# Two maxima over partitions taken by a diagonal, a product with ones and a row maximum; weight splits of small experts moved between three engines

## The chip, the cores and the metric

The kernel runs on one core of a Trainium2 chip. The metric is device time in microseconds of one execution. Engines are named as the profile names them: PE (matrix products; PEld is its weight load), DVE (vector), ACT (scalar), POOL (GpSimd) and SP, whose queue issues most transfers. An engine with a q behind it is its sequencer.

## The reference, cut to what matters

Three stages follow each other: attention with a learned position bias, a mixture of eight experts of which each token takes one, and a dense pair of products.

```python
# attention: B, H, S, D = 2, 8, 576, 64; hidden of the bias = 32
scores = scale * q @ k.T
x = log1p(|i - j|) / log1p(max(i, 1))
scores += (relu(x * w1 + b1) @ w2)            # one bias per head, same for both batches
attn = softmax(scores) @ v
# experts: 1152 tokens of 512, 8 experts, hidden 1024, capacity 288 tokens
e = argmax(x @ w_gate); gate = softmax(x @ w_gate)[e]
y = relu(x_e @ w1[e]) @ w2[e]                 # each expert on its own tokens
out = gate * y
# dense pair, hidden 2048
h = out @ w_in
g = where(h >= 1, h, where(h <= -1, 0, (h + 1)**2 / 4))
return g @ w_out
```

## The kernel before

**The bias, first row block.** A hidden unit of the bias is a kink in x. The kernel turns each kink into a threshold, compares distances with thresholds (`mask_step`, line 244, DVE), and multiplies the masks with two small fp16 tables on PE (`ab_mm`, lines 262 and 263). Of a chunk, DVE scales one half by the table of x (`ab_x`, line 268); ACT copies the other half out (`ab_bs`, line 276, four buffers) and POOL adds it (`ab_add`, line 281), or DVE does both (`ab_stt`, line 286). Each block of 128 rows has 18 chunks. The first block stands alone ahead of the attention, in a loop over `c`; the later blocks are mixed into the attention.

**Two power-of-two scales.** `pow2_scale` takes a maximum over all 128 partitions and turns it into a power of two and its inverse in six small DVE steps. It is called twice. The first call (`sab`) scales the fp16 tables: nothing of the bias can begin before it. Its input `am` is a row maximum of a 128x16 tile (line 619). The second (`sv`) scales v into fp16. Its input `vsum` is made in round 8 of the chunk loop, from three row maxima that ACT takes of v (`v_abs`, line 179); its steps are dealt out over the next rounds. In both, `partition_all_reduce` on POOL (line 117) takes the maximum.

**Around it.** The order on each engine is that of the program text. The constants `cst` (with the unit matrix `ident`), the thresholds' row `lrow`, the distances `sD`, the table `xtab`, and q, k and v are loaded at the start by queues of SP and ACT. After the first scale, DVE scales `lrow` (line 630), ACT takes its exponential and scales `sD` (lines 631 and 632), ACT rounds part of k (`k_hi`, line 153) and POOL takes the rest (`k_lo`, line 159); then come the first mask and the first product.

**The experts.** A weight chunk is 128x1024 values; an expert has eight, four of w1 and four of w2, counted through as `n`. Every chunk is split into a rounded part (`w_hi`) and the rest (`w_lo`, line 888), each in a ring of six. The rounding is a copy on ACT (line 883), for chunks 1 and 3 of each eight on DVE (line 881). The rest is on DVE for even chunks and on POOL for odd ones. `w_lo` also issues the load of chunk `n + 6` on SP's queue. Products take three terms of the two parts.

Each expert has two arms, and the number of its tokens chooses. `small_arm` (at most 128 tokens; lines 1129 and 1140) computes with the tokens stationary, transposes h and y (lines 1116 and 1157), and calls `hook(s)` eight times: `hook(s)` splits chunk 8e + 4 + s, so s = 0 to 3 are this expert's w2 (chunks 4 to 7 of the eight) and s = 4 to 7 the next expert's w1 (chunks 0 to 3). Between hooks 6 and 7 stands `mid()`, where `x_pick` (lines 1179 and 1180, DVE) copies the next expert's tokens to `xsh` and `xsl`; the next small expert's first product waits for these. `wide_arm` (lines 1089 and 1103) takes all 288 columns. In this trace experts 0, 1 and 4 take the wide arm, 2, 3, 5, 6 and 7 the small one.

Of the kernel before, what the change touches and what calls it, by code (L numbers as in the profile page):

```python
# [9 lines left out]
F32 = mybir.dt.float32  # L10
# [6 lines left out]
ALU = mybir.AluOpType  # L17
AX = mybir.AxisListType.X
# [21 lines left out]
    "pp": [12, 10],  # L40
    "HV": (1, 3),
}

P = 128
# [6 lines left out]
def tile_attn_moe_moe2(  # L51
# [6 lines left out]
    nc = tc.nc  # L58
# [14 lines left out]
    const = ctx.enter_context(tc.tile_pool(name="const", bufs=1))  # L73
# [9 lines left out]
    ap1 = attn.enter_context(tc.tile_pool(name="ap1", bufs=1, reuse_waits="tile"))  # L83
# [5 lines left out]
    psM = attn.enter_context(tc.tile_pool(name="psM", bufs=2, space=PSUM, reuse_waits="tile"))  # L89
# [8 lines left out]
    ident = cst[:, 24:24 + P]  # L98
# [8 lines left out]
    def late_consts():  # L107
# [4 lines left out]
        nc.sync.dma_start(out=wg, in_=a["moe_w_gate"].rearrange("(k p) e -> p k e", p=P))  # L112
        nc.sync.dma_start(out=iota, in_=a["c_iota"])

    def pow2_scale(m1, name, pool):
        amax = ap1.tile([P, 1], F32, name=name + "_m")
        nc.gpsimd.partition_all_reduce(amax, m1, P, bass_isa.ReduceOp.max)
        ei = ap1.tile([P, 4], I32, name=name + "_e")
        ef = ap1.tile([P, 4], F32, name=name + "_f")
        sc = const.tile([P, 2], I32, name=name + "_s")  # L120
        s = sc.bitcast(F32)
        steps = [
            lambda: nc.vector.tensor_single_scalar(out=ei[:, 0:1], in_=amax.bitcast(I32), scalar=23, op=ALU.logical_shift_right),
            lambda: nc.vector.tensor_copy(ef[:, 0:1], ei[:, 0:1]),
            lambda: nc.vector.tensor_scalar(out=ef[:, 1:2], in0=ef[:, 0:1], scalar1=64.0, scalar2=-14.0, op0=ALU.max, op1=ALU.add),
            lambda: nc.vector.tensor_scalar(out=ef[:, 2:3], in0=ef[:, 1:2], scalar1=-1.0, scalar2=254.0, op0=ALU.mult, op1=ALU.add),
            lambda: nc.vector.tensor_copy(ei[:, 1:3], ef[:, 1:3]),
            lambda: nc.vector.tensor_single_scalar(out=sc, in_=ei[:, 1:3], scalar=23, op=ALU.logical_shift_left),
        ]
        return s[:, 1:2], s[:, 0:1], steps  # L130

    FH = G["fh"]
    kst = {h: ap1.tile([P, B, S], F32R, name=f"kst{h}") for h in range(H) if h // 2 not in FH}
# [61 lines left out]
    def q_load(it, hp):  # L195
        if hp in FH:
            qraw[it, hp] = ap3.tile([P, 2, P], F32, tag="qf", name="qf")
            nc.sync.dma_start(out=qraw[it, hp], in_=a["qf"][it, hp])
            return
        qraw[it, hp] = ap3.tile([P, 2, B, P], F32, tag="qraw", name="qraw")  # L200
        nc.sync.dma_start(out=qraw[it, hp], in_=a["q"][it, :, 2 * hp:2 * hp + 2])
# [92 lines left out]
    def ab_ev(it, c, dve=False):  # L294
        if dve:
            ab_stt(it, c)
        else:
            ab_bs(it, c)
            ab_add(it, c)
# [292 lines left out]
    with tc.manual_schedule():  # L592
# [9 lines left out]
            nc.sync.dma_start(out=vraw[:, 3 * c:3 * c + 3, :], in_=a["v"][:, 3 * c:3 * c + 3, :])  # L602
        k_load(2)
        q_load(0, 1)
        nc.vector.memset(run, 0.0)
        warm = ap1.tile([P, 1], F32, name="warm")
        nc.vector.memset(warm, 0.0)
# [4 lines left out]
        am = ap1.tile([P, 1], F32, name="am")  # L612
# [4 lines left out]
        V.tensor_scalar(out=ab[:, 1, :], in0=w2r, scalar1=wcol[:, 1:2], scalar2=None, op0=ALU.mult)  # L617
        V.tensor_scalar(out=sg[:, 0:1], in0=sg[:, 0:1], scalar1=-1.0, scalar2=None, op0=ALU.add)
        V.tensor_reduce(out=am, in_=abf, axis=AX, op=ALU.max, apply_absolute_value=True)
        sa, isa, wsteps = pow2_scale(am, "sab", const)  # L620
        V.tensor_scalar(out=sg[:, 1:2], in0=wcol[:, 0:1], scalar1=sg[:, 0:1], scalar2=1e-30, op0=ALU.mult, op1=ALU.max)
        V.reciprocal(out=sg[:, 2:3], in_=sg[:, 1:2])
        wsteps[0]()
        V.tensor_scalar(out=sg[:, 3:4], in0=sg[:, 2:3], scalar1=sg[:, 0:1], scalar2=-1.0, op0=ALU.mult, op1=ALU.mult)
        wsteps[1]()
# [38 lines left out]
        for c in range(NCK + 1):  # L664
            if c < NCK:
                ab_mm(0, c, wide=c % 4 >= 2)
            if 1 <= c <= NCK:
                (ab_xp if G["evx"][c - 1] else ab_x)(0, c - 1)
            if c + 2 < NCK:
                mask_step(0, c + 2)  # L670
            if 1 <= c <= NCK:
                ab_ev(0, c - 1, dve=c in EVD)
            if c in G['va']:
                v_abs(G['va'].index(c))
            if c == 8:
                vsum = ap1.tile([P, 1], F32, name="vsum")
                V.tensor_reduce(out=vsum, in_=vm[:, 0:3], axis=AX, op=ALU.max)
                sv, _, vsteps = pow2_scale(vsum, "sv", const)
                vst["s"] = sv
                vsteps.append(lambda: V.tensor_copy(cvec, sv))  # L680
            if c > 8:
                for f in vsteps[2 * (c - 9):2 * (c - 9) + 2]:
                    f()
            if c == G['pp'][0]:
                v_hi(0)
            if c == G['pp'][1]:
                k_hi(2)
            if c == 1:
                q_hi(0, 0)
                q_lo(0, 0)  # L690
            if c == 8:
                q_hi(0, 1)
            if c == 12:
                late_consts()
                xtab_load(1)
# [133 lines left out]
    NR, NS = 6, 6  # L829
# [44 lines left out]
            w2_dma(n - NCH)  # L874

    HV = G.get('HV', ())

    def w_hi(n):
        if n < NCH:
            if n >= NR and n % 8 in HV:  # L880
                nc.vector.tensor_copy(ring_h[n % NR], stage[n % NS])
            else:
                nc.scalar.copy(out=ring_h[n % NR], in_=stage[n % NS])  # L883

    def w_lo(n, eng=None):
        if n < NCH:
            eng = eng or (nc.gpsimd if n % 2 else nc.vector)
            eng.tensor_tensor(out=ring_l[n % NR], in0=stage[n % NS], in1=ring_h[n % NR].bitcast(F32), op=ALU.subtract)  # L888
            if n < 4:
                pass  # L890
            elif n + NS < NCH:
                w_dma(n + NS)
            elif n % 2:
                w_dma(NCH + (n + NS - NCH) // 2)

    def w_split(n):
        w_hi(n)
        w_lo(n)

    def w1_at(e, c):  # L900
        n = 8 * e + c
# [53 lines left out]
    with tc.manual_schedule():  # L955
# [34 lines left out]
        for n in range(3):  # L990
            w_hi(n)
# [170 lines left out]

    with tc.manual_schedule():
        w_hi(3)
        w_lo(3, nc.gpsimd)
        for n in range(2, 4):
            w_dma(n + NS)
        if CAP == 0:
            zfill_y()
        zx_at = min([e for e in range(E) if e * CAP + WIN > NT], default=E) if CAP else E  # L1170
        if zx_at == 0:
            zfill_x()

        def guess(e):
            if e < E and CAP > P:
                tc.mark_branch_hint_location(f"arm{e}", hint=many[e], engines=[mybir.EngineType.PE])

        def x_pick(r):
            nc.vector.tensor_copy(xsh, xTh[:, :, ds(r["dve"], P)].bitcast(F32))  # L1179
            nc.vector.tensor_copy(xsl, xTl[:, :, ds(r["dve"], P)].bitcast(F32))  # L1180

        done = nx0
        if CAP > 0:
            x_pick(regs[0])
            guess(0)
        for e in range(E if CAP > 0 else 0):
            r = regs[e]
            need = min(NTT, -(-min(NT, (e + 1) * CAP + WIN) // P))
            pre = list(range(NA, nx0)) if e == 0 else []
            more = list(range(done, need))  # L1190
            for t in more:
                if t not in xb:
                    xb[t] = x_gather(t)
            done = max(done, need)

            def hook(s, e=e):
                n = 8 * e + 4 + s
                if n < NCH:
                    w_split(n)
                if NCH - 1 <= n < NCH + 1:  # L1200
                    for k in (0, 1) if n < NCH else (2, 3):
                        w2_decode(0, k)

            def first(pre=pre):
                for t in pre:
                    x_block(t, xb[t])

            def mid(late=True, e=e, first=first, more=more, nxt=regs[e + 1] if e + 1 < E else None):
                if late:
                    first()  # L1210
                for t in more:
                    x_block(t, xb[t])
                if e + 1 == zx_at:
                    zfill_x()
                if e == 1:
                    zfill_y()
                if nxt is not None:
                    x_pick(nxt)

            if CAP > P:  # L1220
                with tc.If(cnts[e] < P + 1, preferred_fallthrough_block=False, label=f"arm{e}") as few:
                    guess(e + 1)
                    small_arm(e, r, hook, mid)
                with few.Else():
                    guess(e + 1)
                    first()
                    wide_arm(e, r, windows, hook, lambda: mid(False))
            else:
                small_arm(e, r, hook, mid)
# [40 lines left out]
    for g in range(4):  # L1270
        lim[0] = 4 * g + 5
        assert not dec or dec[0][0] > 4 * g
        for f in range(4):
            n = (NCH + 4 * g + f // 2) % NR
# [156 lines left out]
```

## Time and profile before

| | |
|---|---|
| median of 3 runs | 683.22 us (682.27 to 684.61) |
| the profiled execution | 680.61 us |
| its span, first to last instruction | 678.8 us |
| mean granted clock of PE | 0.904 of full speed |
| busy over the span | PE 579.8, DVE 501.5, ACT 360.2, POOL 354.0 us |

The first bias block runs from the start to about 50 us, the attention to about 270, the experts from about 292 to 465, the dense pair from there to the end. The profiled execution is 1.8 us longer than its span. A busy PE is not PE at its peak, since matmuls overlap. In a line of the timeline the bracket holds the idle time ahead of the first of its instructions, and what ended it.

### The profile page before, as it was taken

How to read it: one execution, taken by the hardware profiler on the slowest of the kernel's cores; microseconds unless marked ns; L12 is line 12 of the kernel's file. 1: busy time of each engine (PE TensorE's matmuls, PEld its weight loads, DVE VectorE, ACT ScalarE, POOL GpSimd, SP SyncE). 2: the span in 40 equal slices, each digit the busy share in tenths (PEclk: the TensorE clock that was granted, in tenths of full speed). 3: DMA queues.
4: the chain of work that ended last, by engine and by line, in shares of the span. 5: the costliest groups of instructions: out<-in, count | busy, mean ns of one | idle time of the engine just before them, and what ended most of it. 6: DMA issues, size and time to landing. Idle time of an engine off the chain costs nothing.

```text
span 678.8 us, 14201 instructions
## 1 busy us (share of the span) xinstructions
PE 579.8 (85%) x5332; PEld 518.2 (76%) x5332; DVE 501.5 (74%) x948; ACT 360.2 (53%) x761; POOL 354.0 (52%) x279
## 2 busy tenths in 40 slices
PE   1548887997987899499998898888989999999996
PEld 1445766876766788299998898887968988988985
DVE  3749999999989964646468854775895789787432
ACT  2446776787956854343546435543653652652720
POOL 0547998898976862455356553651330330330442
PEclk9655799899979889589999898887979999999998
DMA  9209898989976868575557754764324114200012
GB/s 334 67 3 231 162 158 141 174 153 160 171 159 129 173 109 170 185 271 176 161 190 242 244 181 150 238 207 158 125 72 176 64 63 140 106 3 0 1 47 94
DMA packets 116388, 98.26 MB, mean 145 GB/s; under 512 B 98000, under 2 KB 99024, under 8 KB 114256
## 3 DMA queue, kind: packets, MB, share of 16 engines
q1 hardware_dynamic: 114000, 89.96, 52.5%
q0 software_dynamic: 1440, 4.72, 2.0%
q10 hardware_dynamic: 864, 2.47, 1.1%
q8 instruction: 51, 0.84, 0.5%
q14 instruction: 33, 0.27, 0.1%
HBM read 65.15 MB, written 4.72 MB: 103 GB/s over the span
## 4 chain that ended last, share of the span: by engine, by line
PE 39%; DVE 6%; issue 5%; ACT 3%; POOL 2%; DMA 1%; POOLq 0%; ACTq 0%; DVEq 0%
PE psh L1287 12%; PE psy L1312 7%; PE psh L1089 6%; PE psy L1103 6%; PE psh L1312 5%; PE psh L1129 2%; POOL rl L888 2%; DMA raw<-in_moe_w_dram 1%; ACT rh L883 1%; DVE rt L923 1%; DVE rl L888 1%; DVE gl L1301 1%; DVE cl L1292 1%; POOL out_dram L1320 1%; DVE xsh L1179 1%
## 5 line engine op out<-in xcount | busy, mean ns | idle before, releaser
L888 POOL TENSOR_TENSOR rl<-raw,rh 128x1024 fp32r<-128x1024 f32 x34 | 87.9, 2587 | 94.2 <-ACT rh L883 64.8
L1297 POOL TENSOR_TENSOR rl<-rl,cl 128x384 f32<-128x384 f32 x48 | 51.4, 1071 | 137.1 <-ACT cl L1296 58.5
L262 PE MATMUL ab_ps<-Wt,mask 128*128 128x64 f16 x720 | 63.6, 208 | 53.6 <-ACT bs L276 20.6
L262 PEld LDWEIGHTS <-mask 128*128 128x128 f16 x720 | 54.5, 107 | 42.8 <-DVE mask L244 36.6
L281 POOL TENSOR_TENSOR bias<-bias,bs 128x256 f32<-128x256 f32 x78 | 71.4, 927 | 27.0 <-ACT bs L276 19.6
L392 POOL TENSOR_TENSOR hl<-s,hl 128x576 f16<-128x576 f32 x55 | 78.6, 1432 | 9.8 <-DVE hl L369 3.8
L244 DVE TENSOR_TENSOR mask<-sD,sT 128x1024 f16<-128x1024 f16 x72 | 72.9, 1026 | 0.0
L263 PEld LDWEIGHTS <-mask 128*128 128x128 f16 x720 | 55.2, 108 | 18.0 <-issue 17.9
L1287 PE MATMUL psh<-yTh,rh 128*128 128x384 f32 x192 | 66.3, 345 | 0.7 <-ACT yTh L1159 0.7
L888 DVE TENSOR_TENSOR rl<-raw,rh 128x1024 fp32r<-128x1024 f32 x30 | 47.6, 1586 | 24.5 <-ACT rh L883 16.8
L1287 PE MATMUL psh<-yTh,rl 128*128 128x384 f32 x192 | 65.7, 342 | 0.0
L1287 PE MATMUL psh<-yTl,rh 128*128 128x384 f32 x192 | 64.8, 341 | 0.0
L263 PE MATMUL ab_ps<-Wt,mask 128*128 128x64 f16 x720 | 63.3, 208 | 0.0
L883 ACT CAST rh<-raw 128x1024 fp32r<-128x1024 f32 x50 | 52.2, 1052 | 4.0 <-DMA raw<-in_moe_w_dram 2.2
L276 ACT ACTIVATE bs<-ab_ps,isa 128x256 f32<-128x256 f32 x78 | 35.3, 472 | 32.1 <-DVE bias L268 23.2
L1293 ACT ACTIVATE rl<-psh,half 128x384 f32<-128x384 f32 x48 | 28.0, 583 | 44.3 <-DVE cl L1292 44.2
L1301 DVE TENSOR_TENSOR gl<-rl,gh 128x384 fp32r<-128x384 f32 x48 | 26.8, 557 | 29.1 <-ACT gh L1300 28.6
L359 ACT ACTIVATE s<-s,mn 128x576 f32<-128x576 f32 x56 | 43.5, 776 | 1.7
L345 DVE CUSTOM_DVE_ANT_0 s<-s_ps,bias 128x576 f32<-128x576 f32 x56 | 41.8, 746 | 2.2 <-PE s_ps L317 1.4
L402 PE MATMUL mi<-V16h,pt 128*128 128x64 f16 (+1 forms) x320 | 40.3, 202 | 2.8 <-DMA pt<-hl 2.8
L268 DVE TENSOR_TENSOR bias<-ab_ps,xtab 128x256 f32<-128x256 f32 x88 | 35.6, 415 | 6.6 <-PE ab_ps L263 6.5
L402 PEld LDWEIGHTS <-pt 128*128 128x128 f16 (+1 forms) x320 | 31.4, 107 | 11.8 <-issue 4.3
(256 smaller groups left out, 1998.7 us busy)
## 6 DMA issues: line engine op xcount, KB each, us to landing
raw<-in_moe_w_dram SPq DMA_DIRECT2D x60, 512.0 KB, 4.3
raw<-in_moe_w_in_dram SPq DMA_DIRECT2D x8, 1024.0 KB, 4.8
raw<-in_moe_w_out_dram SPq DMA_DIRECT2D x8, 1024.0 KB, 4.9
qraw<-in_q_dram SPq DMA_DIRECT2D x15, 256.0 KB, 4.3
kst<-kraw SPq DMA_DIRECT2D x12, 288.0 KB, 4.0
vraw<-in_v_dram SPq DMA_DIRECT2D x3, 768.0 KB, 8.1
xd<-xt SPq DMA_DIRECT2D x8, 256.0 KB, 2.0
raw<-in_moe_w_dram ACTq DMA_DIRECT2D x4, 512.0 KB, 7.1
```

The costliest lines, as they stand in the source:

```text
L244: nc.vector.tensor_tensor(out=m, in0=win, in1=thr, op=ALU.is_gt)
L262: nc.tensor.matmul(pv[:, :, j], m[:, j, :], W["h"], start=True, stop=False)
L263: nc.tensor.matmul(pv[:, :, j], m[:, j, :], W["l"], start=False, stop=True)
L281: nc.gpsimd.tensor_tensor(out=bv, in0=bv, in1=bs_t.pop((it, c)), op=ALU.add)
L359: nc.scalar.activation(out=s, in_=s, func=AF.Exp, bias=mn[:, 1:2], scale=0.125, accum_out=st_t[it, h // 2][:, 0, h % 2, b:b + 1])
L392: eng.tensor_tensor(out=hl[:, 1, 0:S], in0=s, in1=hl[:, 0, 0:S], op=ALU.subtract)
L402: nc.tensor.matmul(o, pt[:, blk, ic], vh, start=blk == 0, stop=False)
L883: nc.scalar.copy(out=ring_h[n % NR], in_=stage[n % NS])
L888: eng.tensor_tensor(out=ring_l[n % NR], in0=stage[n % NS], in1=ring_h[n % NR].bitcast(F32), op=ALU.subtract)
L1287: nc.tensor.matmul(ps, l[:, kd, fs], mv[:, kd, cs], start=i == 0, stop=i == 11)
L1297: nc.gpsimd.tensor_tensor(out=rl, in0=rl, in1=cl, op=ALU.add)
L1312: nc.tensor.matmul(ps, l[:, tsl], mv[:, f % 2, :], start=f == 0 and i == 0, stop=f == 3 and i == 2)
```

## The change

`pow2_scale` no longer uses POOL. It multiplies the unit matrix by the column `m1` (a diagonal matrix, DVE), multiplies a matrix of ones with it on PE (every row of the product in PSUM is then the whole column), and takes the maximum of each row (DVE). These three operations are returned as a list and placed by the caller: for `sab` the first two at once and the third after two small steps; for `sv` the first in round 8, the other two in round 9, and the six steps and the copy to `cvec`, which stood in rounds 9 to 12, in rounds 10 to 12.

In the small arm the splits are dealt out anew. Rounding: only chunk 3 on DVE (before 1 and 3), the other seven on ACT. The rest: chunks 5 and 0 on POOL (before 1, 3, 5 and 7), the other six on DVE. The wide arm keeps its deal.

```diff
+    ones = ap1.tile([P, P], F32, name="ones")
+
     def pow2_scale(m1, name, pool):
         amax = ap1.tile([P, 1], F32, name=name + "_m")
-        nc.gpsimd.partition_all_reduce(amax, m1, P, bass_isa.ReduceOp.max)
+        diag = ap1.tile([P, P], F32, name=name + "_d")
+        allm = psM.tile([P, P], F32, tag="mi", name=name + "_p")
+        spread = [
+            lambda: nc.vector.tensor_scalar(out=diag, in0=ident, scalar1=m1[:, 0:1], scalar2=None, op0=ALU.mult),
+            lambda: nc.tensor.matmul(allm, ones, diag, start=True, stop=True),
+            lambda: nc.vector.tensor_reduce(out=amax, in_=allm, axis=AX, op=ALU.max),
+        ]
...
-        return s[:, 1:2], s[:, 0:1], steps
+        return s[:, 1:2], s[:, 0:1], steps, spread
...
+        nc.vector.memset(ones, 1.0)
         nc.vector.memset(run, 0.0)
...
-        sa, isa, wsteps = pow2_scale(am, "sab", const)
+        sa, isa, wsteps, wspread = pow2_scale(am, "sab", const)
+        for f in wspread[:2]:
+            f()
         V.tensor_scalar(out=sg[:, 1:2], ...)
         V.reciprocal(out=sg[:, 2:3], in_=sg[:, 1:2])
+        wspread[2]()
         wsteps[0]()
...
-                sv, _, vsteps = pow2_scale(vsum, "sv", const)
+                sv, _, vsteps, vspread = pow2_scale(vsum, "sv", const)
                 vst["s"] = sv
                 vsteps.append(lambda: V.tensor_copy(cvec, sv))
-            if c > 8:
-                for f in vsteps[2 * (c - 9):2 * (c - 9) + 2]:
+                vspread[0]()
+            if c == 9:
+                vspread[1]()
+                vspread[2]()
+            if c > 9:
+                for f in vsteps[3 * (c - 10):3 * (c - 10) + 3]:
                     f()
...
+    HVS, LPS = (3,), (5, 0)
-    def w_hi(n):
+    def w_hi(n, hv=HV):
         if n < NCH:
-            if n >= NR and n % 8 in HV:
+            if n >= NR and n % 8 in hv:
                 nc.vector.tensor_copy(ring_h[n % NR], stage[n % NS])
...
-    def w_split(n):
-        w_hi(n)
-        w_lo(n)
+    def w_split(n, few=False):
+        if few:
+            w_hi(n, HVS)
+            w_lo(n, nc.gpsimd if n % 8 in LPS else nc.vector)
+        else:
+            w_hi(n)
+            w_lo(n)
...
-            def hook(s, e=e):
+            def hook(s, e=e, few=False):
                 n = 8 * e + 4 + s
                 if n < NCH:
-                    w_split(n)
+                    w_split(n, few)
...
-                    small_arm(e, r, hook, mid)
+                    small_arm(e, r, lambda s: hook(s, few=True), mid)
```

## Rows read from the trace of the kernel before

**Rows 1.** Waits, 0 to 60 us: waiter <- releaser, us, times, longest.

```profile
ACT bs L276 <- POOL bias L281: 6.3, 3, 4.9
...
POOL bias L281 <- issue: 7.1, 1, 7.1
...
DVE sv_e L123 <- POOL sv_m L117: 6.8, 1, 6.8
...
DVE bias L268 <- PE ab_ps L263: 4.6, 2, 3.2
```

**Rows 2.** Timeline of DVE, first bias block: start, duration, line, tiles.

```profile
3.08 0.17 DVE L619 TENSOR_REDUCE am<-ab 128x1 f32<-128x16 f32 x1
...
10.84 0.15 DVE L123 TENSOR_SCALAR sab_e<-sab_m 128x1 int32<-128x1 int32 x1 [7.27 <-POOL sab_m L117]
...
11.53 0.52 DVE L630 TENSOR_SCALAR lrow<-lrow,sg 128x576 f32<-128x576 f32 x1
...
21.11 4.04 DVE L244 TENSOR_TENSOR mask<-sD,sT 128x1024 f16<-128x1024 f16 x2
...
28.88 0.15 DVE L677 TENSOR_REDUCE vsum<-vm 128x1 f32<-128x3 f32 x1 [1.06 <-ACT V16h L179]
...
49.45 0.48 DVE L286 SCALAR_TENSOR_TENSOR bias<-ab_ps,isa,bias 128x256 f32<-128x256 f32 x1
```

**Rows 3.** Instructions of lines 117 and 159, first 60 us: duration, first and last start.

```profile
L117 POOLq MODIFY_POOL_CONFIG  x4: 8/8/13, 1.5 to 30.9; - x4
...
L159 POOLq MODIFY_POOL_CONFIG  x2: 83/83/83, 11.3 to 11.4; - x2
```

**Rows 4.** Timeline of POOL, same stretch.

```profile
20.86 2.61 POOL L159 TENSOR_TENSOR kraw<-kraw 128x1152 fp32r<-128x1152 f32 x1 [9.48 <-ACT bs L276]
```

**Rows 5.** Groups of instructions by shape, whole span: count | busy us, mean ns.

```profile
L317 PE MATMUL s_ps<-kf,qf 64*128 64x288 f32 x64 | 24.3, 529 | 0.0
L473 PE MATMUL gl<-wg,extra 128*128 128x8 f32 x64 | 9.0, 267 | 0.0
...
L434 DVE TENSOR_TENSOR xt<-mi,stat 128x128 f32<-128x128 f32 x4 | 1.2, 292 | 5.7 <-PE mi L408 5.7
```

**Rows 6.** Transfers issued in the first 8 us: KB, us to landing.

```profile
xtab<-in_c_xtab_dram SPq DMA_DIRECT2D x1, 288.0 KB, 4.4
...
cst<-in_c_small_dram ACTq DMA_DIRECT2D x1, 76.0 KB, 2.0
```

**Rows 7.** Windows: length, busy PE PEld DVE ACT POOL, PE clock, DMA, GB/s.

```profile
100.00:150.00 50.00, 44.31 (x704) 36.79 (x700) 49.19 (x99) 37.42 (x98) 46.07 (x39) 0.93 0.91 163
...
429.25:446.65 17.40, 14.54 (x108) 14.09 (x108) 12.64 (x13) 9.61 (x17) 10.51 (x4) 0.90 0.73 244
...
429.10:433.00 3.90, 3.90 (x20) 3.90 (x21) 1.33 (x3) 1.20 (x2) 2.38 (x1) 0.56 0.80 268
```

**Rows 8.** Timeline of DVE, end of small expert 5.

```profile
422.23 2.44 DVE L888 TENSOR_TENSOR rl<-raw,rh 128x1024 fp32r<-128x1024 f32 x1 [0.26 <-ACT rh L883]
424.59 0.68 DVE L881 CAST rh<-raw 128x1024 fp32r<-128x1024 f32 x1
425.19 1.21 DVE L888 TENSOR_TENSOR rl<-raw,rh 128x1024 fp32r<-128x1024 f32 x1
426.33 2.56 DVE L1179 CAST xsh<-xTh 128x512 fp32r x1
```

**Rows 9.** Timeline of POOL, same stretch.

```profile
421.06 2.53 POOL L888 TENSOR_TENSOR rl<-raw,rh 128x1024 fp32r<-128x1024 f32 x1 [0.83 <-ACT rh L883]
425.41 3.20 POOL L888 TENSOR_TENSOR rl<-raw,rh 128x1024 fp32r<-128x1024 f32 x1 [1.82 <-PE psy L1140]
```

**Rows 10.** Timeline of ACT, same stretch.

```profile
421.13 2.02 ACT L883 CAST rh<-raw 128x1024 fp32r<-128x1024 f32 x2
```

**Rows 11.** Timeline of PE: first products of experts 3 and 6.

```profile
365.95 0.36 PE L1129 MATMUL psh<-rh,xsh 128*128 128x256 f32 x1 [1.70 <-DVE xsh L1179]
...
429.03 0.36 PE L1129 MATMUL psh<-rh,xsh 128*128 128x256 f32 x1 [2.58 <-DVE xsh L1179]
```

## Prediction

> **What bounds the kernel now.** I began with the waits of the first 60 us, because two of the three edits lie there. DVE waits 7.27 us for the first maximum [rows 2] and 6.8 for the second; POOL's first add behind the second waits 7.1 for nothing that the profile names, and ACT, whose four copy buffers that add should empty, waits 6.3 in all, 4.9 of it at one place; DVE then waits 4.6 for products that had no bank [rows 1]. What these waits hide shows in the instructions of lines 117 and 159: POOL's sequencer issues a MODIFY_POOL_CONFIG in front of each maximum and again when it goes back to ordinary work, and from the one at 11.3 to the first subtraction at 20.86 POOL does nothing [rows 3, 4], although ACT had rounded its input long before. So each maximum costs two loads of POOL code, one ahead of it and one behind.
>
> The reader is to see in the timeline of DVE that the whole first block hangs on that engine: `am` is there at 3.25 us, its maximum at 10.84, the block ends at 49.93 (49.45 + 0.48) [rows 2]. Then comes the attention, where DVE is busy 49.2 of 50 us and PE 44.3 [rows 7]. I see no work there tied to an absolute time: the order is that of the text, and only the first loads have a clock of their own. So I let what is won before 50 us come through to the end in full.
>
> For the third edit I read the end of small expert 5 on three engines. PE stands idle 2.58 us before expert 6, waiting for `xsh` [rows 11]. DVE makes `xsh` in 2.56 us, from 426.33 to 428.89; POOL's split ran from 425.41 to 428.61 [rows 8, 9]. The same stands at 422.23: a DVE subtraction takes 2.44 us, of which 1.36 lie before POOL's end at 423.59, and 1.08 behind it. The subtraction that met no earlier POOL split took 1.21, and POOL's split behind it 3.20 instead of about 2.4. The two engines take turns, a whole instruction at a time.
>
> **The first maximum.** Removed: a wait of 7.27 us. Added in its place, on the path: a diagonal, a product, a row maximum, and the crossings between engines. The trace of before has none of the three. The diagonal lies between 0.15 us (128x1) and 0.52 (128x576) [rows 2]; I take 0.22, nearer the small one. The fp32 product has 128 columns: 0.27 (8 columns) to 0.53 (288 columns) [rows 5], I take 0.35, which leaves room for either level of the clock. The row maximum reads 128 values from PSUM: 0.17 (16 values from SBUF) [rows 2] to 0.29 for 128x128 from PSUM [rows 5]; I take 0.27. Three crossings at 0.1 each are an estimate from the steps of the DVE chain. Sum 1.1 (0.9 to 1.7), so the six steps begin at about 4.4 instead of 10.84: 6.4 us.
>
> What would be late next are the loads. The unit matrix lands at about 2.7 (0.74 + 2.0), before `am`. `lrow` goes out on SP's queue ahead of `xtab`, which lands 4.4 us after its issue at 1.65 [rows 6], so `lrow` is there by 6.05 at the latest. Line 630, at 11.53 before, would want it at 5.1. If it came only at 6.05, 0.9 is lost. I take **6.2 us** (5.5 to 6.7).
>
> Here a page stands against the change. The Trainium skill, GPSIMD Engine Reference, section 4.1 Engine selection, says that a reduction over partitions belongs on GpSimd. Going by the operation alone, one short instruction would be exchanged for three and two crossings, and the two maxima would cost about 1.5 us more. The trace does not bear that out: what is paid for is the code load [rows 3]. The same reference, section 2.1 Instruction dispatch, gives about 6 us for the first call after a load; row 3 against row 4 gives 9.5 here, while the start's transfers run, so I go by the rows.
>
> If a first load is still due before the first subtraction, it can start when POOL's memsets are done, at about 1.5 us, and at 9.5 us length it is over at 11. Its input, the rounded k, cannot be there before about 8. Three us late would be POOL's, not DVE's, and before it was late by more.
>
> **The second maximum.** Removed: 6.8 us of DVE waiting. Added: diagonal 0.2 and row maximum 0.3 as above, and DVE's wait for PE, which must first finish the sixteen small products of round 9: 0 to 0.85 us by the pace of the block, I take 0.3. The six steps only move by a round. **6.0 us** (5.4 to 6.4).
>
> **The loads behind the maxima.** After the second, POOL's first add goes out 7.1 us late, and DVE loses the 4.6 us in rows 1. Without the load POOL follows each chunk. But its adds then meet DVE's masks, which they did not while POOL loaded: two masks around POOL's subtraction took 4.04 [rows 2]; a mask that meets a short add costs 0.2 more than one that meets nothing, seven times 1.4. I take **3.2 us** (0 to 4.6). After the first maximum the subtraction of k and the adds start earlier, so that ACT falls behind less and DVE's 1.06 us wait for v [rows 2] should go: **1.0 us** (0 to 1.5). The 2.7 us that masks lose to the subtraction (4.04 against two at 0.7) stay; they come at an earlier chunk.
>
> The first block so gives 6.2 + 6.0 + 3.2 + 1.0 = **16.4 us** (10.9 to 19.2).
>
> **The small experts.** Each DVE queue loses one rounding (0.68) and gains two subtractions (1.21 each); POOL loses two of its four splits; ACT gains one rounding of 1.0, in a gap that it has before the end of the expert. Replayed on expert 5: ACT ends chunks 0 and 2 at 422.15 and 423.15 [rows 10]; chunk 1 comes in between, so chunk 2 ends at 424.2. DVE was free at 421.97 [rows 8]; chunk 7's subtraction goes in there, to 423.2. POOL's split of chunk 0 starts when that lets go, at about 422.8, and ends at 425.2. Chunk 1's subtraction waits for that and ends at 426.3, chunk 2's at 427.5, `xsh` at 427.9 instead of 428.89: 1.0 to 1.1 us earlier. The same holds at the end of experts 3 and 6. At the end of expert 2 two evictions of gathered tokens stand on DVE as well, and I see nothing won. In expert 7 the dense pair's decoding no longer waits for POOL: 0.4. Chunk 3's subtraction now stands on DVE ahead of `yTl`, whose bank the next expert's third product group wants; that comes out even, except in the wide expert 4, where I count 1 us lost.
>
> Then the clock. After the 2.58 us pause PE runs 3.9 us at a granted 0.56, part at 1.2 and part at 2.4 GHz [rows 7]: 3.9 x (1 - 0.56) = 1.7 us lost. After the 1.70 us pause of expert 3 [rows 11] no low clock is granted. With pauses of 1.5 us I expect the full clock at experts 4, 6 and 7: 1.5 each.
>
> Sum: 3 x 1.1 + 0.4 - 1.0 + 3 x 1.5 = 7.2; without the clock 3.7 (expert 4's bank wait is then hidden too). I take **6.0 us**. Both bounds of POOL's part go by the six subtractions: if none meets POOL, some 8; if both remaining POOL splits block DVE in full (2 x 2.4) an expert's DVE work is 6 x 1.21 + 0.68 + 4.8 and an estimated 3.5 of evictions and copies, 16.2 us against a period of 17.4 [rows 7], so the edit gives between 1 us per expert and a loss of about as much.
>
> **The sum.** 680.61 - 16.4 - 6.0 = 658.2 for a profiled execution. The median of the runs lies 2.6 above the profiled one, so I forecast **660.8**.
>
> **Rivals.**
>
> *The clock does not follow.* The pauses shrink, but the low clock still comes. The experts give 3.7 instead of 6.0: 663. For it: the low clock begins only some time into the work. Chance 0.2.
>
> *DVE becomes the bound of the small experts.* Everything that needs a split waits behind six subtractions, and each of these stands still while POOL works. The Trainium skill, SBUF — State Buffer, section SBUF: two separate sides, states the rule for it: the pair of ports is locked for a whole instruction, and the other engine blocks. By rows 8 and 9 both remaining splits of POOL then cost DVE up to 2.4, and if `xsh` comes 1 us later in five experts with a low clock behind each: 5 x 1.0 + 1.7 = 7 lost. 683.2 - 16.4 + 7 = 674. Against it: the replay above. Chance 0.12.
>
> *The first block is bounded by something else.* Once the two waits go, loads or the copy buffers hold the block, and only the first maximum and half of the second are won, about 9 us, with 6.0 in the experts: 668. For it: the loads of v and of q are issued behind those of `xtab` and take longer to land [rows 6]. Chance 0.13.
>
> *Slower.* The attention follows the first block with another PE clock. It runs at 0.93 from 100 to 150 us with PE busy 44 of 50 [rows 7]. If the earlier start left PE at the low level through the attention, work of 44 us per 50 would take longer than DVE's 49; at three quarters of the speed 44 becomes 59, 9 us more per 50. From 130 us of such attention on, this exceeds the 22 won; over all 200 us the kernel would end near 699. Against it: the low level was there at 50 us before as well and gave way. Chance 0.03.
>
> *The edits do nothing*, because the code load comes at the next POOL instruction whatever it is and holds the same chain. Then only DVE's two waits change places: within 0.3%, chance 0.02.
>
> **How the numbers follow.** The forecast as described holds 0.5, 660.8 with 654 to 668 from its own terms (19.2 and 8 at best, 10.9 and 3.7 at worst). With the clock rival (inside that), the block rival at 668 and the DVE rival, the range 653 to 672 leaves out part of the DVE rival, the slower case and no change. A difference of 0.3% is 2 us, about what a measurement of this kernel can tell. Faster 0.95, within 0.02, slower 0.03.
>
> **What would show it.** No MODIFY_POOL_CONFIG between the maxima; `sab_e` at 4 to 5 us; the end of the first block at 33 to 35 instead of 49.93 us; the same distance from there to the experts; `xsh` waits of about 1.5 instead of 2.6 us ahead of experts 4, 6 and 7, with clock 1.00 behind them. It is wrong if the block ends later than 40 us, if the attention grows by what the block won, or if the distance from expert 2 to the dense pair grows.

## The result, and the profile after

The changed kernel takes 654.89 us (median of 4 runs, 652.37 to 656.61) against 683.91 for the kernel before in the same session: 0.956 of the time, interval 0.950 to 0.962. The forecast was 660.8 us, range 653 to 672. The profiled execution after is 652.37 us with a span of 650.6; before it was 680.61 and 678.8. So 28.2 us went, where the prediction's sum had 22.4. One profile below, of the kernel in which POOL splits no chunk, is of an execution of 659.84 us, 1.7% above the fastest of that kernel, and only its waits and its DVE durations are read.

Cut at four places, the two profiles say where. The block's end is the end of its last L294 (before: L286). The experts begin at the first L1110 (L1089), and the dense pair at the first product behind expert 7.

| stretch | before | after | gain | predicted |
|---|---|---|---|---|
| start to end of the first block | 49.93 | 33.42 | 16.5 | 16.4 |
| to the first expert product (attention, gathering) | 242.06 | 240.00 | 2.1 | 0 |
| eight experts | 173.10 | 167.23 | 5.9 | 6.0 |
| dense pair to the end | 213.71 | 209.95 | 3.8 | 0 |

The timeline of DVE in the first block after the change (start, duration, line, tiles, idle time before and what ended it):

```profile
3.23 0.17 DVE L628 TENSOR_REDUCE am<-ab 128x1 f32<-128x16 f32 x1
3.44 0.29 DVE L122 TENSOR_SCALAR sab_d<-cst,am 128x128 f32<-128x128 f32 x1
...
4.61 0.29 DVE L124 TENSOR_REDUCE sab_m<-sab_p 128x1 f32<-128x128 f32 x1 [0.56 <-PE sab_p L123]
4.93 0.15 DVE L131 TENSOR_SCALAR sab_e<-sab_m 128x1 int32<-128x1 int32 x1
...
5.63 0.52 DVE L642 TENSOR_SCALAR lrow<-lrow,sg 128x576 f32<-128x576 f32 x1
...
21.59 0.14 DVE L689 TENSOR_REDUCE vsum<-vm 128x1 f32<-128x3 f32 x1
21.76 0.86 DVE L122 TENSOR_SCALAR sv_d<-cst,vsum 128x128 f32<-128x128 f32 x1
...
23.47 0.28 DVE L124 TENSOR_REDUCE sv_m<-sv_p 128x1 f32<-128x128 f32 x1
...
32.94 0.48 DVE L294 SCALAR_TENSOR_TENSOR bias<-ab_ps,isa,bias 128x256 f32<-128x256 f32 x1
```

Both maxima now cost DVE a diagonal, a row maximum, and in the first case 0.56 us of idle time while PE works. The 7.27 us wait and the 1.06 us wait for v [rows 2] are gone; `lrow` was there when L642 wanted it. POOL's sequencer issues a MODIFY_POOL_CONFIG only at 1.8 us, ahead of POOL's first subtraction at 10.49. Of the second maximum's three steps none waits; the 0.86 us of `sv_d` is a 0.2 to 0.3 us operation that met one of POOL's adds.

The small experts, read from the windows of experts 5, 6, 7 and of the pair's first 7 us (length; busy PE, PEld, DVE, ACT, POOL, each with its count of instructions; PE clock; DMA; GB/s), and from PE's timeline at the start of expert 6:

```profile
393.50:408.37 14.87, 13.23 (x109) 12.79 (x109) 10.39 (x11) 10.55 (x18) 5.21 (x2) 1.00 0.50 169
408.37:424.59 16.22, 13.40 (x108) 12.86 (x109) 13.09 (x15) 10.55 (x18) 5.22 (x2) 1.00 0.81 255
424.59:440.65 16.06, 13.59 (x109) 12.87 (x109) 12.62 (x16) 8.56 (x16) 2.54 (x3) 1.00 0.75 276
440.65:447.65 7.00, 7.00 (x40) 7.00 (x41) 4.37 (x9) 2.58 (x5) 1.26 (x2) 1.00 0.19 81
```

```profile
408.37 0.36 PE L1150 MATMUL psh<-rh,xsh 128*128 128x256 f32 x1 [1.34 <-DVE xsh L1200]
...
411.74 0.28 PE L1150 MATMUL psh<-rl,xsh 128*128 128x256 f32 x1 [1.18 <-issue]
```

The pause ahead of expert 6 fell from 2.58 [rows 11] to 1.34 us and the granted clock of its stretch rose from 0.90 [rows 7] to 1.00, as forecast. Expert 5 gained too, with no shorter pause ahead of it: PE waits 2.60 us there, 2.32 before, and its window before the change was

```profile
411.45:429.03 17.58, 14.71 (x108) 14.26 (x109) 11.48 (x11) 9.60 (x17) 8.13 (x3) 0.90 0.46 152
```

What was not forecast either is the second line of PE's timeline: 16 products into expert 6, PE stands for 1.18 us for nothing that the profile names.

### The profile page after: what moved, and what is told of

It reads as the page before. It is cut to its first block, busy times and chain, and to the rows that moved or that the text cites. A ratio compares the mean times of both kernels' runs of the same rounds, so it can differ in the third digit from the quotient of the medians.

```text
span 650.6 us, 14208 instructions
## 1 busy us (share of the span) xinstructions
PE 572.9 (88%) x5336; PEld 509.8 (78%) x5336; DVE 503.9 (77%) x958; ACT 364.2 (56%) x765; POOL 330.3 (51%) x268
## 4 chain that ended last, share of the span: by engine, by line
PE 53%; DVE 23%; issue 9%; ACT 5%; DMA 2%; POOL 2%; POOLq 0%; DVEq 0%; SPq 0%; ACTq 0%
PE psh L1308 12%; PE psy L1333 7%; PE psh L1110 6%; PE psy L1124 6%; DVE mask L252 5%; PE psh L1333 5%; PE psh L1150 5%; DVE s L353 3%; DVE bias L276 3%; PE s_ps L336 2%; ACT rh L900 2%; DMA pt<-hl 1%; PE mi L410 1%; PE s_ps L325 1%; PE ab_ps L270 1%
## 5 line engine op out<-in xcount | busy, mean ns | idle before, releaser
L905 POOL TENSOR_TENSOR rl<-raw,rh 128x1024 fp32r<-128x1024 f32 x25 | 63.6, 2549 | 110.3 <-ACT rh L900 84.3
L270 PE MATMUL ab_ps<-Wt,mask 128*128 128x64 f16 x720 | 62.8, 206 | 28.7 <-ACT bs L284 14.9
L905 DVE TENSOR_TENSOR rl<-raw,rh 128x1024 fp32r<-128x1024 f32 x39 | 60.1, 1548 | 17.1 <-PE psh L1150 8.4
L270 PEld LDWEIGHTS <-mask 128*128 128x128 f16 x720 | 52.9, 106 | 22.9 <-DVE mask L252 17.4
L271 PEld LDWEIGHTS <-mask 128*128 128x128 f16 x720 | 54.0, 107 | 13.8 <-issue 13.8
L271 PE MATMUL ab_ps<-Wt,mask 128*128 128x64 f16 x720 | 62.4, 206 | 0.0
L900 ACT CAST rh<-raw 128x1024 fp32r<-128x1024 f32 x54 | 55.9, 1054 | 4.2 <-DMA raw<-in_moe_w_dram 2.3
L411 PE MATMUL mi<-V16l,pt 128*128 128x64 f16 (+1 forms) x320 | 39.7, 200 | 0.7 <-DVE V16l L194 0.7
L949 ACT CAST rh<-rt 128x512 fp32r<-128x512 f32 (+1 forms) x31 | 19.4, 636 | 37.3 <-DVE rt L946 37.3
```

Of the source, the lines that this page charges most:

```text
L270: nc.tensor.matmul(pv[:, :, j], m[:, j, :], W["h"], start=True, stop=False)
L271: nc.tensor.matmul(pv[:, :, j], m[:, j, :], W["l"], start=False, stop=True)
```

## Experiments

### The two halves alone

```diff
 # only_max: the changed kernel, splits of before
-                    small_arm(e, r, lambda s: hook(s, few=True), mid)
+                    small_arm(e, r, hook, mid)
 # only_split: the kernel before, with HVS, LPS and few of the changed one
```

> Both maxima by the diagonal, the small experts' splits as in the kernel before. If the two halves of the change are independent, the first block ends at 33.4 us, the experts take the 172.4 us of before with waits for xsh of 2.6 us ahead of experts 4, 6 and 7, and the pair behind them starts at the low clock: 683.4 - 16.5, with the 2 us that attention lost 667 to 669. Rival: the clock in the experts and at the pair's start is a matter of the run or of the earlier start and not of the splits: then 2 to 6 us less, 661 to 665, with the granted clock at 1.00 behind expert 3.

> Both maxima by POOL as before, the small experts' splits as in the changed kernel. If the splits give the clock back, the experts take 166 to 167 us instead of 172.4 and the pair 210 instead of 213.7: 683.4 - 5.9 - 3.8, 673 to 675. Attention stays at the 204.07 us of before if what it lost in the changed kernel is the maxima's doing. Rival: the splits are worth only the shorter pauses (3 times 1.2 us less the new wait of 1.1 us for yTl), 680 to 681, and the clock does not follow.

(The first text adds 2 us, the second speaks of a loss, for an attention that became longer; by the table above that stretch became 2.1 us shorter.) Measured: the maxima alone 663.14 us, 0.971 (0.964 to 0.977); the splits alone 674.77 us, 0.989 (0.983 to 0.995). Windows of experts 5 to 7 and of the pair's start, the maxima alone:

```profile
403.68:421.21 17.53, 14.74 (x109) 14.30 (x109) 11.24 (x11) 9.65 (x17) 8.02 (x3) 0.90 0.47 152
421.21:438.84 17.63, 14.75 (x109) 14.31 (x109) 12.88 (x14) 9.60 (x17) 10.53 (x4) 0.90 0.77 241
438.84:457.07 18.23, 15.08 (x108) 14.36 (x108) 12.06 (x14) 8.57 (x16) 7.43 (x5) 0.91 0.69 231
457.07:464.07 7.00, 7.00 (x40) 7.00 (x41) 4.37 (x9) 2.58 (x5) 1.25 (x2) 1.00 0.18 75
```

and the splits alone:

```profile
415.40:431.63 16.23, 14.74 (x109) 14.30 (x109) 10.19 (x11) 10.64 (x18) 5.06 (x2) 0.89 0.47 154
431.63:447.65 16.02, 13.41 (x108) 12.87 (x109) 13.08 (x15) 10.56 (x18) 5.21 (x2) 1.00 0.80 259
447.65:463.71 16.06, 13.60 (x108) 12.88 (x108) 12.61 (x16) 8.56 (x16) 2.54 (x3) 1.00 0.76 276
463.71:470.71 7.00, 7.00 (x31) 7.00 (x32) 2.85 (x6) 1.38 (x3) 1.02 (x1) 0.76 0.19 81
```

Experts 6 and 7 take 16 us at clock 1.00 with the new splits and 17.6 and 18.2 at 0.90 and 0.91 with the old ones, whether the block is short or long. So in these profiles this part of the gain goes with the splits, and the rival that an earlier start brings the clock back is not borne out for the experts. Two things hold that back. The profile of the maxima alone is of an execution of 670.05 us at a mean granted clock of 0.910; three others took 660.82 to 663.14 us at 0.916 to 0.927, the median lies where the rival had it (661 to 665), and no trace shows the experts there. And for the pair the rival stands: with the old splits its first 7 us ran at 1.00 as well.

### One maximum at a time

```diff
+        if name == "sv":       # only_second: "sab"
+            spread = [lambda: nc.gpsimd.partition_all_reduce(amax, m1, P, bass_isa.ReduceOp.max),
+                      lambda: None, lambda: None]
```

> The first maximum by the diagonal, the second by POOL, splits as changed. If each use of POOL's operation costs a load of code ahead of it and one behind it, the second maximum alone costs its own 6.0 and the 3.2 us of the load behind it: the first block ends at 42 to 43 us instead of 33.4, the whole is 663 to 665 us. Rival: only the first use of the operation loads something and a later one is cheap: the block ends below 37 us, 655 to 658 us.

> The first maximum by POOL, the second by the diagonal, splits as changed. By the prediction's terms the first maximum costs 6.2 and the load behind it 1.0 us: the block ends at 40 to 41 us instead of 33.4, 661 to 663 us. Rival: the first use of POOL's operation carries nearly all of the 16.5 us: the block ends above 46 us, 668 to 672 us.

The block ends at 41.94 us with the second maximum on POOL and at 40.91 with the first: 8.5 and 7.5 us more than 33.42, together 16.0 of the 16.5 us that both cost. Both rivals (that the first use carries all, or that the later one is cheap) fall: each maximum on POOL is paid in full. The whole took 668.06 us, 0.982 (0.976 to 0.988), and 667.77 us, 0.974 (0.966 to 0.982), above the 663 to 665 and 661 to 663 expected; the attention is too uneven to read single microseconds from the whole (below). POOL's timeline with the second maximum on POOL:

```profile
20.78 1.74 POOL L291 TENSOR_TENSOR bias<-bias,bs 128x256 f32<-128x256 f32 x2
28.15 0.38 POOL L127 PARTITION_ALL_REDUCE sv_m<-vsum  x1 [5.63 <-issue]
35.99 1.39 POOL L291 TENSOR_TENSOR bias<-bias,bs 128x256 f32<-128x256 f32 x2 [7.46 <-issue]
```

0.38 us of work stand between 5.63 and 7.46 us in which POOL does nothing. Each of the two stretches begins as POOL's sequencer issues MODIFY_POOL_CONFIG:

```profile
L127 POOLq MODIFY_POOL_CONFIG  x2: 6/6/6, 22.5 to 22.5; - x2
...
L291 POOLq MODIFY_POOL_CONFIG  x2: 82/82/83, 28.5 to 28.5; - x2
```

Both kernels have the new splits, and in both PE waits 1.34 us ahead of expert 6. Even so that expert did not get the full clock, as its windows show, with the second maximum on POOL:

```profile
417.62:434.02 16.40, 14.75 (x109) 14.31 (x109) 13.12 (x15) 10.55 (x18) 5.22 (x2) 0.90 0.73 247
```

and with the first:

```profile
422.83:440.96 18.13, 15.92 (x109) 15.39 (x109) 12.02 (x15) 10.63 (x18) 4.80 (x2) 0.81 0.75 240
```

### The load without the wait

```diff
+                junk = ap1.tile([P, 1], F32, name="junk")
+                nc.gpsimd.partition_all_reduce(junk, vsum, P, bass_isa.ReduceOp.max)
                 vspread[0]()
```

> The changed kernel with one POOL maximum of vsum more in round 8, which nobody reads: DVE waits for nothing, so what the time grows by is POOL standing still for its loads. In the run with the second maximum by POOL the loads took 5.6 us ahead of the operation and 7.5 us behind it. If POOL's adds are what the end of the first block hangs on, the block ends 8 to 10 us later than the 33.4 us of the changed kernel, as with the maximum read (42 to 43); if DVE's wait for the result was what cost, the block ends within 3 us of 33.4.

The block ends at 42.57 us, 9.15 us later than in the changed kernel, although `sv_e` starts at 24.35 us, no later than there, and nobody reads `junk`. The whole: 666.69 us, 0.980 (0.974 to 0.987). The timeline of POOL, then that of DVE:

```profile
28.27 0.76 POOL L694 PARTITION_ALL_REDUCE junk<-vsum  x1 [5.52 <-DVE bias L276]
36.63 0.71 POOL L289 TENSOR_TENSOR bias<-bias,bs 128x256 f32<-128x256 f32 x1 [7.60 <-issue]
```

```profile
24.35 0.14 DVE L131 TENSOR_SCALAR sv_e<-sv_m 128x1 int32<-128x1 int32 x1
...
38.95 0.42 DVE L276 TENSOR_TENSOR bias<-ab_ps,xtab 128x256 f32<-128x256 f32 x1 [9.22 <-PE ab_ps L271]
```

and two of the waits of its first 60 us, between them:

```profile
ACT bs L284 <- POOL bias L289: 11.3, 1, 11.3
...
PE ab_ps L270 <- ACT bs L284: 10.8, 2, 9.9
```

POOL's adds stand still, ACT finds no free copy buffer, PE no free bank (the part of PSUM that a product is written to), and DVE no product. So POOL's standing still is as dear when DVE does not wait for the result. The other way round, DVE's wait without POOL's standing still, was not run.

### Filling the pause

```diff
+        for _ in range(16):   # behind L1178, in the kernel with the maxima alone
+            nc.tensor.matmul(psY[0][:, 0:256].rearrange("p (i t) -> p i t", i=2), hTh[:, 0, 0:P],
+                             hTh[:, 0:2, 0:P], start=True, stop=True)
```

> Both maxima by the diagonal, the splits of before, and behind the last transposes of each small expert 16 products of 128x256 whose result is not used: TensorE works through about 1.9 us of its 2.6 us wait for xsh. If it is the pause that costs the clock, experts 6 and 7 take 16.2 to 16.8 us instead of 17.5 and 18.2 with the granted clock at 1.00, and the pair starts at 1.00: 656 to 660 us against the 663 us of the same kernel without the products. If the clock fell for another reason, experts 6 and 7 stay at 17.5 to 18.2 us and the whole at 662 to 668 us.

666.56 us, 0.978 (0.970 to 0.987), so neither faster nor clearly slower than the 663 us without the products, and within the 662 to 668 expected if the clock fell for another reason. Windows of experts 6 and 7:

```profile
418.98:435.13 16.15, 15.14 (x124) 14.73 (x125) 12.79 (x14) 9.72 (x17) 10.56 (x4) 1.00 0.79 261
435.13:454.27 19.14, 16.66 (x124) 16.25 (x125) 12.74 (x14) 8.56 (x16) 7.32 (x3) 0.91 0.70 249
```

Expert 6 agrees with the theory of the pause (16.15 us at 1.00 with the old splits, 17.63 at 0.90 without the products), expert 7 does not. Time was also lost ahead of them: PE waits 4.92 us for nothing named ahead of expert 2, which no other profile has, and expert 1, with that wait at its end, took 37.36 us (30.15 without the products); why this came with them is open. One expert speaks for the theory, the other and the total against it, and what is said of the clock rests on the comparison of splits above.

### What the remaining pause is made of

The rounding of chunk 1 back to DVE; and, the other way, no chunk for POOL:

```diff
-    HVS, LPS = (3,), (5, 0)
+    HVS, LPS = HV, (5, 0)     # hi_as_before: HV is (1, 3)
+    HVS, LPS = (3,), ()       # lps_none
```

> The changed kernel, with the rounding of chunk 1 back on DVE, as before the change; the rests stay with POOL for chunks 5 and 0 only. If DVE's queue ahead of xsh is what counts, 0.7 us more of it makes the pause before xsh 2.0 us, and the clock of experts 6 and 7 is lost in part: 16.7 to 17.5 us each, half of the experts' gain. Rival: the gain is all in POOL's two chunks fewer: pauses of 1.3 us and 16.0 to 16.2 us.

> The changed kernel, with POOL splitting no chunk of a small expert: DVE does all eight. In the changed kernel the pair of chunks ahead of xsh took 4.12 us on DVE while POOL's chunk 0 ran, against 2.4 for two such chunks alone. If POOL's chunk holds DVE's, three chunks on DVE alone take 3.6 us, the pause before xsh shrinks from 1.3 to about 0.8 us, and experts 6 and 7 take 15.6 to 16.2 us. Rival: DVE's own work becomes the bound (two chunks of 1.21 us more for each expert), the pauses grow and experts 6 and 7 take 17 to 18 us.

With one rounding of 0.7 us more on DVE: 663.88 us, 0.972 (0.964 to 0.981), against 0.963 (0.954 to 0.973) for the changed kernel in the same session. Ahead of experts 6 and 7 PE waits 1.91 and 1.80 us for `xsh` instead of 1.34, and the windows of experts 5 to 7 read:

```profile
401.91:418.83 16.92, 14.72 (x108) 14.27 (x109) 11.04 (x12) 9.70 (x17) 5.06 (x2) 0.90 0.49 161
418.83:435.70 16.87, 14.77 (x108) 14.33 (x109) 13.55 (x16) 9.70 (x17) 4.94 (x2) 0.90 0.79 251
435.70:451.75 16.05, 13.59 (x108) 12.86 (x108) 12.61 (x16) 8.56 (x16) 2.55 (x3) 1.00 0.73 258
```

The pauses came as expected, the time only at expert 6; expert 7 took the rival's 16.05 us at 1.00. In this profile the eight experts take 174.24 us, as much as before the change (173.10). So in this profile POOL's two chunks fewer are not enough alone; the intervals of the two totals overlap.

With POOL out of it: **651.22 us**, 0.951 (0.943 to 0.958), the fastest median of all; in the same session the changed kernel took 657.60, 0.963 (0.954 to 0.973), so that its lead is likely and not certain. DVE's timeline at the end of expert 5, of the changed kernel:

```profile
403.76 4.12 DVE L905 TENSOR_TENSOR rl<-raw,rh 128x1024 fp32r<-128x1024 f32 x2
407.81 0.41 DVE L1200 CAST xsh<-xTh 128x512 fp32r x1
```

with POOL's last chunk beside it:

```profile
402.85 2.81 POOL L905 TENSOR_TENSOR rl<-raw,rh 128x1024 fp32r<-128x1024 f32 x1 [2.01 <-ACT rh L900]
```

and of the kernel without POOL's chunks:

```profile
408.77 3.48 DVE L905 TENSOR_TENSOR rl<-raw,rh 128x1024 fp32r<-128x1024 f32 x3
412.18 0.42 DVE L1200 CAST xsh<-xTh 128x512 fp32r x1
```

Three chunks on DVE alone take less than two that meet one of POOL's. The Trainium skill says in SBUF — State Buffer, section SBUF: two separate sides, that GpSimd and VectorE share a port pair which one instruction locks as a whole. The trace agrees: of DVE's 4.12 us, 1.90 pass until POOL's chunk ends at 405.66, and both subtractions fit into the 2.22 us behind it. The rival that the prediction built on this rule, DVE as the bound, fell, because taking POOL's chunks over costs DVE less than waiting for them. PE's timeline of expert 6 in this kernel:

```profile
412.89 0.35 PE L1150 MATMUL psh<-rh,xsh 128*128 128x256 f32 x1 [0.15 <-issue]
...
418.64 0.28 PE L1150 MATMUL psh<-rh,xsl 128*128 128x256 f32 x1 [3.48 <-issue]
```

The pause for `xsh` is gone (about 0.8 us of it was expected to stay), and a nameless one of 3.48 us stands in the expert instead.

### The pause taken away by order

`xsh` and `xsl` are copied behind the last `hTl`, ahead of the chunks; in the second kernel chunk 3 is also split behind `yTl`:

```diff
             if f == 0:
                 tr(3)
+                pick()                  # x_pick(next), where no block is gathered
-            if f in HK:
+            if f in HK and f != HK[3]:  # the second kernel; hook(7) stands behind yTl
```

> The changed kernel, with the copy to xsh and xsl put right behind the last hTl, ahead of the chunks that DVE splits, in the experts that gather no more blocks. If those chunks are what holds xsh, the 1.3 us ahead of experts 6 and 7 go; the subtraction to yTl, still behind chunk 3, then comes later than TensorE wants its bank, and 1 us comes back as a wait in the third chunk of the next expert: 652 to 656 us, about as before this edit. Without that wait 650 to 652 us.

> As the kernel with the early copy, and chunk 3 of the next expert split behind the subtraction to yTl instead of ahead of it. If the bank was the next wait, the experts lose all their pauses of over 0.5 us, three or four of 1.3 us: experts 6 and 7 at 14.8 us, 648 to 652 us. If chunk 3 now comes too late, TensorE waits for it in the fourth chunk and the time is that of the changed kernel, 653 to 657 us.

660.70 us, 0.970 (0.961 to 0.979), and 659.02 us, 0.967 (0.958 to 0.975): neither beats the changed kernel, and both lie above the times expected. PE's timeline, first kernel, expert 6:

```profile
416.73 0.36 PE L1150 MATMUL psh<-rh,xsh 128*128 128x256 f32 x1 [0.16 <-issue]
...
421.75 0.39 PE L1150 MATMUL psh<-rh,xsh 128*128 128x256 f32 x1 [3.00 <-issue]
```

and the DMA queues of its 418 to 422 us (packets, MB, share):

```profile
q1 hardware_dynamic: 330, 1.21, 91.6%
q8 instruction: 1, 0.02, 1.5%
```

The pause went as expected. The wait for the bank was 0.3 us at expert 7, not 1; at expert 6 `yTl` was written while PE stood in the nameless wait, which took 3.0 us there (2.33 in the second kernel). Set side by side, pause ahead of expert 6 and nameless wait inside it were 2.58 and none (before), 1.34 and 1.18 (changed), 0.16 and 3.00, 0.15 and 3.48. The other profiles do not all follow: 1.34 us of pause came with 0.83 (changed, again), with 0.98 (first maximum on POOL) and with none (second on POOL), 0.74 with none where the pause was filled, and expert 7 had pauses of 0.06 us and no such wait. In the two longest a transfer of the instruction queue lies within the wait, while the weights' transfers filled the DMA engines; in the changed kernel one lies ahead of it, between 409 and 410 us. The kernel before has such a transfer in expert 6 too, at 433.1 us, and no wait. That PE's next instructions are what came late is my reading and not shown; what the rows show is that in these two kernels and in the one without POOL's chunks the nameless wait took back what the pause gave up.

### The same kernels once more

> The kernel before, unchanged, for a second profile: if attention's length is a matter of the run, it differs from the 204.07 us of the first profile by some us either way; the experts and the first block must not differ by over 1 us (experts 172.4 us, block end 49.9). If the 4 us by which attention was shorter in the changed kernel belong to the change, attention is within 1 us of 204.07.

> The changed kernel, unchanged, for a second profile and more rounds: the block ends at 33.4 us again; attention is 200 to 210 us if it is a matter of the run, 200.05 within 1 us if it is not; the experts take 166 to 167 us where the clock stays at 1.00 and up to 1.5 us more for each expert where it does not. 650 to 662 us.

The kernel before took 687.88 us in its one execution; the changed one 657.60 us, 0.963 (0.954 to 0.973). The windows from the block's end to the last attention score, kernel before again, changed kernel, changed kernel again:

```profile
49.35:261.73 212.38, 188.50 (x2549) 154.51 (x2547) 191.72 (x405) 148.86 (x374) 174.40 (x146) 0.80 0.83 155
```

```profile
33.42:235.53 202.11, 175.93 (x2546) 145.19 (x2544) 193.75 (x404) 148.17 (x374) 175.14 (x145) 0.87 0.90 162
```

```profile
33.44:238.18 204.74, 178.36 (x2548) 147.35 (x2547) 192.59 (x405) 148.22 (x374) 175.17 (x145) 0.86 0.87 159
```

| profile | block end | to first expert | experts | pair | PE clock, whole |
|---|---|---|---|---|---|
| before | 49.93 | 242.06 | 173.10 | 213.71 | 0.904 |
| before, again | 49.35 | 249.59 | 173.29 | 213.87 | 0.888 |
| the splits alone | 49.87 | 246.44 | 167.40 | 212.79 | 0.904 |
| the maxima alone | 33.82 | 247.71 | 175.54 | 211.13 | 0.910 |
| changed | 33.42 | 240.00 | 167.23 | 209.95 | 0.928 |
| changed, again | 33.44 | 242.52 | 170.08 | 210.06 | 0.923 |
| first by diagonal | 41.94 | 239.59 | 170.04 | 210.13 | 0.919 |
| second by diagonal | 40.91 | 247.02 | 169.09 | 210.18 | 0.905 |
| load without wait | 42.57 | 240.84 | 170.05 | 210.14 | 0.914 |

Block and splits repeat over the profiles of this table: the block within 0.6 us for the same maxima, the experts 173.1 to 175.5 with the old splits and 167.2 to 170.1 with the new. The stretch to the first expert does not: it is 242.06 and 249.59 us in two profiles of one kernel, and 239.6 to 247.7 with a short block. The work is the same (DVE 191.7 to 194.3 us busy), the clock 0.80 in the longest against 0.86 and 0.87; it does not explain all of it, since the first profile of before took 206.13 us at 0.87. The 2.1 us there are no effect that can be told from what one kernel shows by itself.

## Why the prediction was right, step by step

**The first maximum.** Right in size: 7.5 us against 6.2 + 1.0. `sab_e` came 5.9 us earlier, so 1.6 us of the 7.5 lie behind it, where I had 1.0. From `sab_d` to `sab_e` it took 1.49 us, not 1.1: the fp32 product is two records on PE, 3.78 to 4.57 us, where I had 0.35, and diagonal and row maximum took 0.29 each (0.22 and 0.27). `sab_e` came at 4.93 where 4.4 was forecast.

**The second maximum and the load behind it.** The sum is right, 8.5 us against 6.0 + 3.2, but the two terms are not two things. I priced DVE's wait at 6.0 and the load at 3.2. The run with the load and no reader shows that the load costs 9.15 without DVE's wait: had the wait been taken away and the load left, I would have forecast 6 us and got none. The step that was wrong is that of reading each wait of the list as a cost of its own; in that run the waits of ACT, PE and DVE are one chain, from POOL's standing still.

**The objection of the page.** The Trainium skill, GPSIMD Engine Reference, section 4.1 Engine selection, sends partition maxima to GpSimd. Here two on DVE and PE saved 16.5 us, because POOL's 0.38 us operation brought 5.6 to 9.3 us of standing still ahead of it and 7.1 to 9.6 behind it. Where POOL already runs such operations back to back, no run here says anything.

**The small experts.** 5.9 against 6.0 in this pair of profiles, 3 to 8 over all of them. The replay held: `xsh` came 1.2 us earlier. Pauses were 1.34 where I wrote 1.5, and the wide expert lost 1.1 us to `yTl`, forecast as 1. The clock's part of the sum came out by luck. I counted it at experts 4, 6 and 7, behind pauses that became shorter. Expert 5, which I did not count, got the full clock behind a pause of 2.60 us, and with the shorter pause at its end went from 17.58 to 14.87 us; against that experts 0 and 1 took 1.6 us more and expert 6 lost 1.18 to the nameless wait. With the new splits expert 6 ran at 1.00 in four of the six profiles of the table and expert 7 in five, with the old splits in none of three; but behind the same 1.34 us expert 6 ran at 0.90 and 0.81 as well. So the length of the pause ahead does not by itself settle the clock, what else does is open, the rival "the clock does not follow" was not wrong everywhere, and part of the gain differs from run to run.

**What the sum left out.** The dense pair, 3.8 us. My mechanism would give it through a start at full clock, which I did not carry past expert 7; but the start does not settle it. The changed kernel, again, began the pair at 0.76 (first 7 us) and took 210.06 us all the same, and the maxima alone began it at 1.00 and gained 2.6. What goes with its length is the clock of the whole pair, 0.96 before and 0.99 in both profiles of the changed kernel. Its windows, before, then changed, again:

```profile
465.09:678.80 213.71, 205.18 (x1008) 186.48 (x1008) 148.82 (x244) 96.40 (x183) 60.24 (x57) 0.96 0.21 73
```

```profile
446.04:656.10 210.06, 201.47 (x1008) 183.55 (x1008) 148.87 (x244) 96.48 (x183) 60.17 (x57) 0.99 0.21 74
```

The pair took 210.0 to 210.2 us in five of the six profiles with the new splits in the table and 212.8 in the sixth, 211.1 to 213.9 in the three with the old, and 211.2 to 213.5 in four profiles of further variants: how much of the 3.8 belongs to the change stays open.

With the 2.1 us of the attention these 3.8 are the 5.9 by which 654.89 lies below 660.8. The terms as added up did not reach that far: 19.2 + 8 at best, taken from 683.2, is 656.0 and not the 654 that I wrote, so that the lower end of the range holds the result by the room left in it and not by a term.

**Rivals.** The bound of the first block by something else fell, and so did edits that do nothing (the block ended at 33.42). DVE as the bound of the experts fell (with all chunks on DVE the median was the lowest). A slower attention did come in some profiles, but in the kernel before too.

## What to carry to other kernels

When an engine issues a configuration ahead of one odd operation and again behind it, cost the operation by the engine's idle time on both sides and follow that one hole through the buffers that it starves; adding up the waits of all the engines behind it counts the same hole several times. Two engines that lock each other out can be slower together than one alone, so try the split with one of them taken out. And when a pause is shortened, look at what was going on unseen in it: here a wait of PE's own in some profiles, and a clock that changed between profiles, took or gave as much as the pause itself.

## What the runs showed of the hardware

Three things I had not expected. PE's nameless wait inside an expert: 1.18 us with a pause of 1.34 ahead of it, 3.48 with one of 0.15, none with 2.58, but none with 1.34 either in one profile. The attention of one unchanged kernel: 206.13 and 212.38 us, at mean granted clocks of 0.87 and 0.80. And with 0.7 us of work per expert moved from ACT to DVE, the eight experts took 174.24 us in the one profile of it, against 167.2 to 170.1: about 0.5 us more of pause, and a granted clock of 0.90 in experts 5 and 6.
